# Queries turned in 32 by 32 blocks by VectorE instead of TensorE, with the order of the later batches written anew

## The chip, the cores and the metric

The kernel runs on one core of one Trainium2 chip. The metric is the device time of one execution in microseconds (us): the median of several runs, less is better. A core has five engines that each work through their own queue in order and meet only at semaphores: TensorE (PE in the profile, with its weight loads as PEld), VectorE (DVE), ScalarE (ACT), GpSimd (POOL) and SyncE (SP), which here issues nearly all DMAs.

## The reference

Two stages, all float32. First an attention through packs: 8 batches, 8 heads, 576 tokens, 64 depths, and 32 pack queries for each head.

```python
p_packed = sm_attn(p, k, v)                 # 32 packs attend to 576 tokens
out = sm_attn(q, p_packed, p_packed)        # 576 queries attend to the 32 packs
x = out.transpose(0, 2, 1, 3).reshape(B, S, H * D)
xt = x.transpose(0, 2, 1)
u = x + (xt @ U @ V).transpose(0, 2, 1)     # token mixing of rank 32
ch = np.maximum(u @ w_ch1, 0.0) @ w_ch2     # 512 -> 2048 -> 512
return u + ch
```

`sm_attn` is a softmax of `qk/8` with 1e-9 added to the sum, times the values.

## The kernel before, in words

The packs' attention over all batches comes first (the word list `opening`), mixed with the loading of weights and the first batch's products. Then batch 1 is run by a plain loop, and batches 2 to 7 by three lists of words: `prologue` once, `batch_steps` for each batch, `joint_steps` after batches 3 and 7 for the rows that four batches share. Each word names a stage and takes that stage's next piece; the program order of every engine's queue comes out of the order of these words. Nothing else orders the work: a piece whose inputs are not there holds up everything behind it on its engine.

Within a batch `batch_steps` weaves three things:

- The two large products of this batch. `H` (`half1`, lines 95 to 97) makes hidden values: six matmuls of 256 or 320 columns. `E` and `L` move them out of PSUM on ScalarE. `U` (lines 1016 to 1018) makes sums on VectorE, `C` (line 1030, ScalarE) and `D` (line 1035, VectorE) split them into a high and a low part in one of two tiles `h`, and `G` (`products`, line 1041) multiplies the parts with weights: 21 matmuls of 256 columns for a turn of four `G`. One factor of each turn, the tile `tc`, is brought from DRAM each time (`P`, line 936) into one of two rooms; the DMA waits until the turn before last has let the room go.
- The weights of the coming batch, `F0` (line 564, TensorE), `F1` and `F2` (lines 574 and 576, ScalarE and VectorE), from the tile `w1s` that `S` loads (line 556).
- The attention of the coming batch, `q..`, `s..`, `t..`, `x..`, `y..`. Its queries come in two groups of four heads (`g` is 0 or 1). For each group `load_nat` fills one tile `x`: nine tokens on a row, 64 depths each, 576 KB in one DMA (line 292). `q0`, `q1` and `q2` (`turn`, lines 303 and 306) turn them on TensorE through the identity into PSUM banks: four, four and two transposes of 128 columns. `q0a`, `q1a` and `q2a` (lines 312 and 314) copy them to the tile `xT` on ScalarE, depths on partitions. `s3` (line 323) multiplies `xT` with the packs, `s4` (line 365) turns the 32 by 32 blocks of the scores on VectorE, `s5` to `s9` are the softmax on VectorE, GpSimd and ScalarE, and `sa` (line 389) turns the result back on VectorE. There is one buffer of `xT`, which also serves `t0`, and beside the tile that a weight keeps there is one buffer of `x` for queries and for `t0` in turn.

Of the kernel before, what the change touches and what calls it, by code (L numbers as in the profile page):

```python
# [9 lines left out]
F32 = mybir.dt.float32  # L10
# [10 lines left out]
def packed_attention_mixer_kernel(  # L21
# [27 lines left out]
    nc = tc.nc  # L49
    B, H, S, D = q.shape  # L50
    NP = p.shape[2]
    R = U.shape[1]
    DM = H * D
    DF = w1.shape[1]
    P = 128
    SM = 512
    NT = 9
    I = S // NT
# [7 lines left out]
    LAST = slice(4 * I, 5 * I)  # L66
# [4 lines left out]
    U, V, w1, w2 = (a.bitcast(I32) for a in (U, V, w1, w2))  # L71
# [28 lines left out]
    pipe = ctx.enter_context(tc.tile_pool(name="pipe", bufs=1))  # L100
# [3 lines left out]
    def bank():  # L104
        return psT.tile([P, 512], F32, name="t_ps", tag="t")
# [8 lines left out]
    for z in range(2):  # L114
        a, b = (x[:, D:].rearrange("p (y z n) -> p z y n", y=2, z=2) for x in (swapped, ident))
# [15 lines left out]
    def ppT_tile():  # L131
        return pipe.tile([P, 2, P], F32, name="ppT", bufs=3)
# [4 lines left out]
    def load_ppT(b):  # L137
        ppT[b] = ppT_tile()
        nc.sync.dma_start(out=ppT[b].rearrange("p g n -> p (g n)"), in_=ppTd[b])
# [86 lines left out]
    def x_tile():  # L226
        return pipe.tile([P, 5 * 2 * P], F32, name="x", tag="x", bufs=2)
# [63 lines left out]
    def load_nat(x, src, b, g):  # L291
        nc.sync.dma_start(
            out=x.rearrange("p (h y) -> p h y", h=2),
            in_=src[b, 4 * g:4 * g + 4].rearrange("(h z) (i c) d -> (z i) h (c d)", z=2, c=NT))

    def turn(x, h, bank):

        x = x.rearrange("p (h y) -> p h y", h=2)
        t_ps = bank()
        if h < 2:  # L300
            pairs = t_ps.rearrange("p (k y a) -> p k y a", k=2, a=2)
            for j in range(4):
                nc.tensor.transpose(pairs[:, j % 2, :, j // 2], x[:, h, P * j:P * j + P], ident)  # L303
        else:
            for h in range(2):
                nc.tensor.transpose(t_ps[:64, P * h:P * h + P], x[:, h, SM:], ident)
        return t_ps
# [26 lines left out]
    def attention(b, res):  # L334

        st = {}

        def load():
            load_q(0)
            if b < 3:  # L340
                load_q(1)
            if b > 0:
                load_ppT(b)

        def load_q(g):
            st["x", g] = x_tile()[:, :2 * S]
            load_nat(st["x", g], q, b, g)

        def turn_q(g, h):
            st["t_ps", g, h] = turn(st["x", g], h, bank)  # L350
# [105 lines left out]
        def run(f, *args):  # L456
            return lambda: f(*args)

        if b != 2:
            gh = list(product(range(2), range(2)))  # L460
            return {
                "a0": [load], "a1": [run(load_q, 1)],
                **{f"q{h}": [run(turn_q, g, h) for g in range(2)] for h in range(3)},
                **{f"q{h}a": [lambda scalar, g=g, h=h: turned_q(g, h, scalar) for g in range(2)] for h in range(3)},
                "s3": [run(scores_q, g) for g in range(2)],
                "s4": [run(side, g, r) for g, r in gh],
                "s5": [run(most, g) for g in range(2)],
                "s6": [run(each, g, "m", ALU.subtract) for g in range(2)],
                "s7": [run(power, g) for g in range(2)],
                "s8": [run(total, g, k) for g in range(2) for k in range(3)],  # L470
                "s9": [run(each, g, "s", ALU.mult) for g in range(2)],
                "sa": [run(back, g) for g in range(2)],
                "t0": [room],
                "t1": [run(tokens, k) for k in (0, 2, 4)],
                "t2": [run(split_tokens, k, False) for k in (0, 2, 4)],
                "t3": [run(split_tokens, k, True) for k in (0, 2, 4)],
                "x0": [mix1], "x1": [run(split_mix1, False)], "x2": [run(split_mix1, True)],
                "y0": [run(mix2, g, hf) for hf, g in gh],
                "y1": [run(add_mix2, g, hf) for hf, g in gh],
                "y2": [run(high_mix2, g, hf) for hf, g in gh],  # L480
                "y3": [run(low_mix2, g, hf) for hf, g in gh],
                "pu": [put],
            }
# [674 lines left out]
    for word in opening.split():  # L1158
        name = word.rstrip("v") if word not in stages else word
# [7 lines left out]
        else:  # L1167
            stage()
    ahead = attention(2, res)
    ahead.pop(0)()  # L1170
    steps = ahead
    last = kept["cur"]
    now = Batch(1)
    for kt in range(NK):
# [11 lines left out]
        if kt % 4 == 2:  # L1186
            n = NPC + kt // 4 + 1
# [13 lines left out]
        c, y = divmod(kt - 1, 2)  # L1201
# [10 lines left out]
    last = now  # L1212

    prologue = (
        "a0 XG XG Hn Hn Ln En Hn En X U Ln F0n X X V C XG XMv Pn F1n XG V Sn En V Zn Hn XMv X V Hn En XMv F1n F1n Hn "
        "F2n Ln En F2n XMv Hn En Ln F2n F1n Hn En F2n Wn D En Wn U XO XO Pn XO XO Yn "
    )
    batch_steps = (
# [9 lines left out]
    )  # L1228
    joint_steps = (
# [3 lines left out]
    )  # L1233

    def each_of(f, *items):
# [4 lines left out]
    sweeps, rows = {}, {}  # L1240
# [58 lines left out]
    def run(order, without=""):  # L1299
        for word in order.split():  # L1300
            name = word if word in stages else word[:-1]
            if name[-1] == without:
                continue
            stage = next(stages[name], None)
            if stage:
                stage(*([name == word] if name in either else []))
# [40 lines left out]
```

## Time and profile before

| what | us |
|---|---|
| median of 3 runs | 778.45 (777.95 to 779.28) |
| the profiled execution | 776.24 |
| its span, first to last instruction | 774.5 |

The profile is of one execution. Its views give engine, line, operation and tiles; a busy time is the union of an engine's instructions. Matmuls overlap in the pipeline, so the time that one costs is read from the distance of starts in the timeline, not from its duration. The granted clock of TensorE was 0.997 of full speed over the span.

### The profile page before, as it was taken

Reading aid. Unit: us, or ns where it says so; the run is one execution under the profiler, and the core shown is the slowest. Engines: PE = TensorE matmul, PEld = TensorE weight load, DVE = VectorE, ACT = ScalarE, POOL = GpSimd, SP = SyncE. Lnnn points to the kernel's source line nnn. Section 1 sums busy time; section 2 is a strip of 40 time slices with the busy share of each in tenths; the row PEclk is TensorE's granted clock in tenths of the full one; section 3 lists DMA queues with packets and bytes.
Section 4 is the critical chain, followed back from the end, with each engine's and each line's share of the span. In section 5 each row is a group of like instructions: output and inputs, shape, how many; then the busy total and the mean of one; then the engine's idle time right before and its main releaser. Section 6 shows DMA issues by size and latency. Waiting matters only on the chain.

```text
span 774.5 us, 18505 instructions
## 1 busy us (share of the span) xinstructions
PE 758.3 (98%) x7280; PEld 669.7 (86%) x7280; DVE 571.4 (74%) x1209; ACT 416.4 (54%) x1034; POOL 88.3 (11%) x109
## 2 busy tenths in 40 slices
PE   8999999999999999999999999999999999999996
PEld 6666778787878899899999989998999999999996
DVE  4799799976878657856788758865886578656786
ACT  4788755553434555556554554555555555564441
POOL 1023011010101011200210002010202020200000
PEclk9999999999999999999999999999999999999998
DMA  9999985477122774566567546654656464555581
GB/s 316 346 350 297 314 213 151 124 250 255 39 82 104 244 258 107 190 206 200 164 220 224 194 143 186 195 200 152 213 146 245 149 204 146 197 176 164 164 218 61
DMA packets 105685, 151.18 MB, mean 195 GB/s; under 512 B 40448, under 2 KB 59904, under 8 KB 102016
## 3 DMA queue, kind: packets, MB, share of 16 engines
q1 hardware_dynamic: 105440, 149.75, 61.7%
q8 instruction: 57, 0.93, 0.5%
q10 hardware_dynamic: 160, 0.26, 0.1%
q14 instruction: 28, 0.23, 0.1%
HBM read 116.29 MB, written 33.69 MB: 194 GB/s over the span
## 4 chain that ended last, share of the span: by engine, by line
PE 82%; DVE 8%; ACT 4%; DMA 3%; issue 1%; POOL 0%; SPq 0%; ACTq 0%; DVEq 0%; POOLq 0%
PE o L1041 32%; PE h_ps L95 9%; PE h_ps L96 8%; PE h_ps L97 8%; PE t_ps L564 4%; PE o L95 3%; PE o L97 3%; PE o L96 3%; DVE h L1035 2%; PE o L1063 1%; PE t_ps L303 1%; DMA kx<-in_k_dram 1%; DMA bits<-in_moe_w_ch_dram 1%; PE t_ps L323 1%; ACT h L1030 1%
## 5 line engine op out<-in xcount | busy, mean ns | idle before, releaser
L1041 PE MATMUL o<-w2h,h 128*128 128x256 f32 x896 | 180.4, 281 | 0.0
L95 PE MATMUL h_ps<-ah,wth 128*128 128x256 f32 (+1 forms) x512 | 157.9, 308 | 0.4 <-ACT hj L785 0.4
L96 PE MATMUL h_ps<-al,wth 128*128 128x256 f32 (+1 forms) x512 | 150.6, 294 | 0.0
L97 PE MATMUL h_ps<-ah,wtl 128*128 128x256 f32 (+1 forms) x512 | 150.4, 294 | 0.0
L1035 DVE TENSOR_TENSOR h<-bits,h 128x896 fp32r<-128x896 f32 (+1 forms) x112 | 118.9, 1062 | 37.4 <-ACT h L1030 35.3
L1041 PEld LDWEIGHTS o<-w2h,h 128*128 128x128 f32 x896 | 146.3, 188 | 0.1
L1030 ACT CAST h<-bits 128x896 fp32r<-128x896 f32 (+1 forms) x112 | 100.4, 896 | 62.8 <-DVE bits L1018 31.5
L1041 PE MATMUL o<-w2l,h 128*128 128x256 f32 x448 | 125.3, 280 | 0.0
L95 PEld LDWEIGHTS h_ps<-ah,wth 128*128 128x128 f32 x512 | 96.3, 188 | 24.8 <-issue 10.1
L96 PEld LDWEIGHTS h_ps<-al,wth 128*128 128x128 f32 x512 | 96.4, 188 | 0.9
L97 PEld LDWEIGHTS h_ps<-ah,wtl 128*128 128x128 f32 x512 | 96.3, 188 | 0.0
L1041 PE MATMUL o<-tb,h 128*128 128x256 f32 x504 | 88.1, 281 | 0.9 <-DVE h L1035 0.9
L576 DVE TENSOR_TENSOR wtl<-t_ps,wth 128x256 fp32r<-128x256 f32 x128 | 49.4, 417 | 50.3 <-ACT wth L574 49.4
L1041 PEld LDWEIGHTS o<-w2l,h 128*128 128x128 f32 x448 | 84.2, 188 | 0.0
L1041 PEld LDWEIGHTS o<-tb,h 128*128 128x128 f32 x504 | 71.9, 189 | 2.1 <-DVE h L1035 1.7
L1006 ACT ACTIVATE bits<-h_ps 128x256 f32<-128x256 f32 x132 | 48.3, 388 | 39.4 <-PE h_ps L97 24.6
L1016 DVE TENSOR_TENSOR bits<-bits 128x256 f32<-128x256 f32 x96 | 41.4, 431 | 26.4 <-ACT bits L1006 26.3
L574 ACT CAST wth<-t_ps 128x256 fp32r<-128x256 f32 x128 | 43.3, 378 | 25.8 <-PE t_ps L564 21.1
L373 POOL TENSOR_TENSOR e<-e,m 128x576 f32<-128x576 f32 x16 | 22.7, 1418 | 286.5 <-DVE m L369 286.5
L454 POOL TENSOR_TENSOR al<-aT,ah 128x320 fp32r<-128x320 f32 (+1 forms) x32 | 32.9, 1040 | 182.8 <-ACT ah L450 154.7
L95 PE MATMUL o<-w2h,h 128*128 128x512 f32 x128 | 51.9, 406 | 0.0
L97 PE MATMUL o<-w2h,h 128*128 128x512 f32 x128 | 50.4, 394 | 0.0
(176 smaller groups left out, 1332.9 us busy)
## 6 DMA issues: line engine op xcount, KB each, us to landing
w1s<-w1D SPq DMA_DIRECT2D x24, 1024.0 KB, 6.2
tc<-tD SPq DMA_DIRECT2D x94, 256.0 KB, 3.0
bits<-in_moe_w_ch_dram SPq DMA_DIRECT2D x32, 512.0 KB, 4.6
kx<-in_k_dram SPq DMA_DIRECT2D x16, 576.0 KB, 6.4
x<-in_q_dram SPq DMA_DIRECT2D x16, 576.0 KB, 6.9
vt<-in_v_dram SPq DMA_DIRECT2D x32, 256.0 KB, 6.4
out_dram<-os SPq DMA_DIRECT2D x32, 256.0 KB, 2.8
hD<-ppall SPq DMA_DIRECT2D x30, 256.0 KB, 3.3
```

What stands on the lines that cost most here:

```text
L95: nc.tensor.matmul(ps, lhsT=lh, rhs=rh, start=start, stop=False)
L96: nc.tensor.matmul(ps, lhsT=lh, rhs=rl, start=False, stop=False)
L97: nc.tensor.matmul(ps, lhsT=ll, rhs=rh, start=False, stop=stop)
L454: nc.gpsimd.tensor_tensor(al[:, g, ns], aT[:, ns], ah[:, g, ns].bitcast(F32), op=ALU.subtract)
L564: nc.tensor.matmul(f_ps[g][xs], lhsT=ppT[b][zs, g, xs], rhs=w[zs, h // 2], start=True, stop=True)
L574: nc.scalar.copy(hi[:, g], src)
L576: nc.vector.tensor_tensor(lo[:, g], src, hi[:, g].bitcast(F32), op=ALU.subtract)
L1006: nc.scalar.activation(dst[:, 256 * (i % 2):256 * (i % 2) + 256], src, AF.Relu)
L1016: vec(l[:, 4:6], s[:, 1:3], s[:, 0:1].to_broadcast([P, 2, P]), op=ALU.add)
L1030: nc.scalar.copy(h[:, ks], src)
L1035: nc.vector.tensor_tensor(lo[:, ks], src, h[:, ks].bitcast(F32), op=ALU.subtract)
L1041: nc.tensor.matmul(ps, lhsT=a, rhs=b, start=x not in self.begun, stop=last and i == 2)
```

## The change

For batches 3 to 7 `load_blocks` replaces `load_nat`. It reads queries in pieces of one token by 32 depths (128 bytes) and lays them so that each quarter of 32 partitions holds tokens on its rows and 32 depths in its columns. A group is loaded in four steps `n`, a step in four DMAs of 256 pieces, and in the first two steps one more for the tokens that are ninth in their row: 18 DMAs a group, each of 256 pieces of 128 bytes, where one DMA of 256 pieces of 2304 bytes was before. `turn_blocks` then turns the 32 by 32 blocks on VectorE straight from `x` to `xT`: two instructions of 128 partitions by 512 elements (`qt`) and one of 64 partitions by 256 (`q9`) for each group. The transposes on TensorE, their PSUM banks and the copies on ScalarE fall away in these batches. The softmax and all products stay. Batches 0 to 2 keep the old way.

```diff
+    def load_blocks(x, b, g, n):
+        src = q[b, 4 * g:4 * g + 4].rearrange("h (f l c) (y d) -> c y l h f d", f=4, c=NT, y=2)
+        main = src[:8].rearrange("(a k r) y l h f d -> r y k a l (h f) d", a=2, k=2)
+        r, y = divmod(n, 2)
+        ps = x[32 * n:32 * n + 32]
+        for k, a in product(range(2), range(2)):
+            to = ps[:, 4 * P * k:4 * P * k + 4 * P].rearrange("(l a) (n d) -> a l n d", a=2, d=32)
+            nc.sync.dma_start(out=to[a], in_=main[r, y, k, a])
+        if r == 0:
+            rows = q[b, 4 * g:4 * g + 4].rearrange("h (f l c) (y d) -> c y l (h f) d", f=2, c=NT, y=2)
+            nc.sync.dma_start(out=ps[:, 8 * P:].rearrange("l (n d) -> l n d", d=32), in_=rows[8, y])
...
-        def load_q(g):
-            st["x", g] = x_tile()[:, :2 * S]
-            load_nat(st["x", g], q, b, g)
+        def load_q(g, n=0):
+            if b < 3:
+                x = st["x", g] = x_tile()[:, :2 * S]
+                load_nat(x, q, b, g)
+                return
+            if n == 0:
+                st["x", g] = x_tile()
+                if g == 0:
+                    load_ppT(b)
+            load_blocks(st["x", g], b, g, n)
+
+        def turn_blocks(g, last):
+            x = st["x", g]
+            if not last:
+                st["t", g] = pipe.tile([P, 4, 5 * I], F32, name="xT", bufs=1)
+                for k in range(2):
+                    nc.vector.transpose(st["t", g][:, :, P * k:P * k + P],
+                                        x[:, 4 * P * k:4 * P * k + 4 * P].rearrange("p (h n) -> p h n", h=4))
+            else:
+                nc.vector.transpose(st["t", g][:I, :, LAST], x[:I, 8 * P:].rearrange("p (h n) -> p h n", h=4))
...
-                "a0": [load], "a1": [run(load_q, 1)],
+                "a0": [load] if b < 3 else [run(load_q, 0, n) for n in range(4)],
+                "ql": [run(load_q, 1, n) for n in range(4)],
+                "qt": [run(turn_blocks, g, False) for g in range(2)], "q9": [run(turn_blocks, g, True) for g in range(2)],
...
-        "q0 H C H L G L q0a G E G E P U G N F0 N D H S H E H E F1 H F2 F1 E N F1 F2 L G F2 L C G q1 E P D H W H E F1 "
+        "H H N C N G N F0 L L D E E G U F1 F1 G N H qt H E q9 G E N H N F2 O F2 H E L P H L F1 W G F2 F1 E ql G E U C "
...
+        "G G D H S F2 Y H P E C H E L s3 L E G s4 G s4 H N P N H ql s5 E H D s6 E G L U E s7 G ql s8 G F0 s8 ql H F1 "
+        "F2 F1 G F1 F2 C W G P F1 D H L E H U L E F2 G E L U G C G F2 G s8 P qt s9 G O Plj H q9 C W D H D E s3 E A U "
```

All three lists are written anew. The first group's loads (four words `a0`) move into the end of the batch before, the second group's (four words `ql`) stand between the first group's `q9` and the second group's `qt`.

TensorE, in the batch that prepares batch 3, at the second group's queries. Before, the transposes of `q0` and `q1` stand between two products of one turn (`tb` and `tc` are weights, `h` the split values, `t_ps` the PSUM banks):

```order
L1041 MATMUL o<-w2h_120,h 128x256
L1041 MATMUL o<-tb_3389,h 128x256 x3
L303 MATMUL t_ps<-ident,x 128x128 x8
L1041 MATMUL o<-tc,h 128x256 x3
L1041 MATMUL o<-tb_3389,h 128x256 x3
```

After, TensorE meets that group only at its scores (L335 is line 323 of before, L1071 is 1041, L1093 is 1063):

```order
L97 MATMUL h_ps<-ah,wtl 128x320
L335 MATMUL t_ps<-xT,ppT 32x320
L335 MATMUL t_ps<-xT,ppT 32x256
...
L1093 MATMUL o<-ppP,aP 128x64 x16
L1071 MATMUL o<-tb_3389,h 128x256 x3
L1071 MATMUL o<-tc,h 128x256 x3
```

The eight transposes are gone from between the products, and no matmul has come in their place.

VectorE, in the same batch, at the first group. Before, sums (`bits`), the split (`h`) and the weights' low parts (`wtl`) follow each other until the scores are turned (L365):

```order
L1016 TENSOR_TENSOR bits<-bits 128x256
L1017 TENSOR_TENSOR bits<-bits 128x128
L1018 TENSOR_TENSOR bits<-bits 128x128
L1035 TENSOR_TENSOR h<-bits,h 128x896
L576 TENSOR_TENSOR wtl<-t_ps,wth 128x256 x3
L1035 TENSOR_TENSOR h<-bits,h 128x896
```

After, the queries' blocks are turned between the sums and the low parts (L1046 to L1048 are the sums, L606 is 576, L1065 is 1035):

```order
L1046 TENSOR_TENSOR bits<-bits 128x256
L1047 TENSOR_TENSOR bits<-bits 128x128
L1048 TENSOR_TENSOR bits<-bits 128x128
L372 STREAM_TRANSPOSE xT<-x 128x4x128 x2
L375 STREAM_TRANSPOSE xT<-x 64x4x64
L606 TENSOR_TENSOR wtl<-t_ps,wth 128x256 x3
L1046 TENSOR_TENSOR bits<-bits 128x256
L1047 TENSOR_TENSOR bits<-bits 128x128
L1048 TENSOR_TENSOR bits<-bits 128x128
L1065 TENSOR_TENSOR h<-bits,h 128x896
```

Three instructions have come in that write `xT`; three low parts, three sums and one split queue behind them.

SyncE, in the same batch, at the second group's loads. Before, one DMA loads the group between the stores of hidden values and the weights' stream:

```order
L963 DMA hjD_112<-aP 128x4x64
L1009 DMA hD_106<-ppall 128x512
L292 DMA x<-in_q_dram 128x2x576
L556 DMA w1s<-w1D_102 128x2048
L1009 DMA hD_106<-ppall 128x512
L936 DMA tc<-tD_139 128x512
```

After, the first step's five DMAs stand ahead of `w1s`, and thirteen more follow in one piece after two `tc` (L303 and L306 here are the DMAs of `load_blocks`; L966 is 936, L586 is 556, L1039 is 1009):

```order
L1039 DMA hD_106<-ppall 128x512
L303 DMA x<-in_q_dram 16x16x32 x4
L306 DMA x<-in_q_dram 32x8x32
L586 DMA w1s<-w1D_105 128x2048
L993 DMA hjD_112<-aP 128x4x64
L966 DMA tc<-tD_137 128x512
L966 DMA tc<-tD_138 128x512
L303 DMA x<-in_q_dram 16x16x32 x4
L306 DMA x<-in_q_dram 32x8x32
L303 DMA x<-in_q_dram 16x16x32 x8
L1039 DMA hD_106<-ppall 128x512
L966 DMA tc<-tD_139 128x512
```

Eighteen issues stand where one stood, and `w1s`, `tc` and the store `hD` queue behind them.

More of the change, by code (lines that the diff above doesn't have):

```diff
@@ L339, in load @@
             load_q(0)
-            if b < 3:
-                load_q(1)
+            load_q(1)
             if b > 0:
                 load_ppT(b)
-        def load_q(g):
-            st["x", g] = x_tile()[:, :2 * S]
-            load_nat(st["x", g], q, b, g)
+        def load_q(g, n=0):
[17 more added lines that the diff above has]
+                nc.vector.transpose(st["t", g][:I, :, LAST], x[:I, 8 * P:].rearrange("p (h n) -> p h n", h=4))
         def turn_q(g, h):
@@ L1214, in packed_attention_mixer_kernel @@
     prologue = (
-        "a0 XG XG Hn Hn Ln En Hn En X U Ln F0n X X V C XG XMv Pn F1n XG V Sn En V Zn Hn XMv X V Hn En XMv F1n F1n Hn "
-        "F2n Ln En F2n XMv Hn En Ln F2n F1n Hn En F2n Wn D En Wn U XO XO Pn XO XO Yn "
+        "a0 Hn Hn Ln F0n En XG Ln En Sn F1n U Zn Hn F1n X Hn F2n C XG En D F1n XG X En XG X V F1n V Hn V X Pn V Wn Hn "
+        "F2n Ln En XMv a0 Hn F2n Ln En F2n Hn En XMv XMv En a0 XMv U a0 Pn XO Wn XO XO XO Yn "
     )
     batch_steps = (
[9 rows of a table removed]
[9 rows of a table added]
     )
     joint_steps = (
[3 rows of a table removed]
[3 rows of a table added]
     )
```

20 rows, old and new, of tables (batch_steps, joint_steps) are left out of this document.

## The prediction

> **What bounds the kernel now.** I read the page's busy times first, then a table of stretches of 50 us, then the chain that ended last.
>
> ```profile
> PE 758.3 (98%) x7280; PEld 669.7 (86%) x7280; DVE 571.4 (74%) x1209; ACT 416.4 (54%) x1034; POOL 88.3 (11%) x109
> ...
> PE 82%; DVE 8%; ACT 4%; DMA 3%; issue 1%; POOL 0%; SPq 0%; ACTq 0%; DVEq 0%; POOLq 0%
> ```
>
> ```profile
> core 0: us, PE busy (x) PEld busy (x) DVE busy (x) ACT busy (x) POOL busy (x), PEclk, DMA share, GB/s
> 250.00:300.00 50.00, 50.00 (x441) 44.78 (x440) 32.93 (x72) 27.24 (x76) 4.19 (x3) 1.00 0.70 222
> ...
> 400.00:450.00 50.00, 49.61 (x495) 46.86 (x494) 38.53 (x88) 23.93 (x55) 4.29 (x4) 1.00 0.69 218
> ...
> 650.00:700.00 50.00, 50.00 (x456) 45.94 (x455) 32.41 (x71) 27.14 (x71) 4.30 (x4) 1.00 0.58 185
> ```
>
> A busy PE is not yet a PE at its peak, since matmuls overlap. But 82% of the chain lies on it, and where the change acts (from about 260 us on) it is idle for 0.4 us in the worst of these stretches, at the full clock (1.00). VectorE is busy 32 to 39 of 50 us there, ScalarE 24 to 27, the DMA engines 58 to 70% of the time. So what is taken out of TensorE's queue comes off the end, as long as nothing else arrives later than now.
>
> **What the change removes.** The transposes after 240 us are those of batches 3 to 7:
>
> ```profile
> L303 PE MATMUL t_ps<-ident,x x80: 271/272/273, 262.1 to 629.9; 128*128 128x128 f32 x80
> ```
>
> Their duration of 272 ns is not their price. That is read from the starts in TensorE's timeline (start, duration):
>
> ```profile
> 272.21 0.60 PE L303 MATMUL t_ps<-ident,x 128*128 128x128 f32 x4
> 272.57 0.36 PE L95 MATMUL h_ps<-ah,wth 128*128 128x256 f32 x1
> 272.77 0.28 PE L96 MATMUL h_ps<-al,wth 128*128 128x256 f32 x1
> 272.89 0.28 PE L97 MATMUL h_ps<-ah,wtl 128*128 128x256 f32 x1
> ...
> 275.86 0.38 PE L306 MATMUL t_ps<-ident,x 128*64 128x128 f32 x2
> 275.99 0.36 PE L1041 MATMUL o<-w2h,h 128*128 128x256 f32 x1
> 276.20 0.28 PE L1041 MATMUL o<-w2l,h 128*128 128x256 f32 x1
> ```
>
> ```profile
> 289.81 1.03 PE L303 MATMUL t_ps<-ident,x 128*128 128x128 f32 x8
> 290.60 0.48 PE L1041 MATMUL o<-tc,h 128*128 128x256 f32 x2
> ```
>
> Four transposes hold the queue from 272.21 to 272.57, 0.36 us. The matmul behind them then takes 0.20 until the next starts, where an undisturbed one takes 0.12 (272.77 to 272.89): going from float32 to the split kind costs 0.08 more. So a group of four costs 0.44. Two of L306 cost 0.13 and 0.09 (275.99 to 276.20 less 0.12), 0.22. Eight in one piece cost 0.79, and 0.08 behind them, 0.87. A batch has two fours, one eight and two pairs: 2 x 0.44 + 0.87 + 2 x 0.22 = 2.19 us. Five batches (80 transposes of the first kind, 16 in each) make 10.95, say 11.0 us. Of the matmuls that stay, none is added, and the other places where float32 and split products meet keep their number.
>
> The Trainium skill, page "TensorE: Matmul & The Clock Gate", section "Back-to-back issue gap", gives about 81 ns for a sustained weight load and matmul of 128 columns; by that the hundred would be worth 8.1 us. The rows give 90 ns in a group and the 0.08 behind it, and I go by the rows.
>
> The copies on ScalarE go too, and the queries stop using PSUM banks:
>
> ```profile
> L312 ACT COPY xT<-t_ps 128x512 f32<-128x512 f32 x30 | 17.2, 592 | 15.3 <-PE t_ps L303 15.0
> L314 ACT COPY xT<-t_ps 64x256 f32<-64x256 f32 x16 | 5.8, 365 | 3.0 <-PE t_ps L306 2.9
> ```
>
> Four of 592 ns and two of 365 are 3.1 us of ScalarE in a batch. It is half idle; I count nothing for this.
>
> **What it adds on VectorE.** For each group two turns of 128 x 512 and one of 64 x 256. The nearest rows:
>
> ```profile
> L389 DVE STREAM_TRANSPOSE aT<-e 128x576 f32<-128x576 f32 x16 | 12.3, 771 | 7.6 <-POOL e L373 7.5
> ...
> L365 DVE STREAM_TRANSPOSE e<-t_ps 128x256 f32<-128x256 f32 x16 | 6.5, 406 | 0.0
> ```
>
> L389 also goes from SBUF to SBUF: 512/576 of 771 is 0.69 us; two of L365 would be 0.81, the upper end. The small one lies between 256/576 of 771, 0.34, and 0.41. I take 0.69 and 0.36: 1.7 us a group, 3.5 a batch, 17 in all (20 by the upper ends). In 50 us that is about 2.2 more, and 38.5 becomes 40.7: VectorE doesn't become the bound by its sum. It also has gaps that such a piece fits into:
>
> ```profile
> 266.25 0.43 DVE L1016 TENSOR_TENSOR bits<-bits 128x256 f32<-128x256 f32 x1 [2.33 <-ACT bits L1006]
> ...
> 278.44 0.85 DVE L365 STREAM_TRANSPOSE e<-t_ps 128x320 f32<-128x320 f32 x2 [2.79 <-PE t_ps L323]
> ```
>
> I cost it at nothing. The cover is these gaps; if it is gone, up to 1.7 us a group lands on TensorE (first rival). The change also adds a wait there: the turn waits for the last DMA of its group, and the low parts L576, the sums L1016 and the split L1035 queue behind it. TensorE waits for the split (`G`) and the low parts (`H`).
>
> **What it adds on SyncE and the DMA engines.** Eighteen issues a group for one:
>
> ```profile
> L950 SPq DMA_DIRECT2D ppP<-ppD x24: 303/430/1157, 260.2 to 685.7; - x24
> DMA to landing us min/median/max: 1.8/2.2/5.6
> ```
>
> ```profile
> L292 SPq DMA_DIRECT2D x<-in_q_dram x10: 469/539/2548, 251.3 to 620.8; - x10
> DMA to landing us min/median/max: 5.7/6.0/7.7
> ```
>
> L950, 32 KB in pieces of 256 bytes, is nearest: 0.43 us an issue, so 7.7 a group and 15.5 a batch, less 1.1 for the two of L292. SyncE mostly waits. One row alone:
>
> ```profile
> SPq L936 <- PE o L1041: 143.4, 58, 7.1
> ```
>
> So there is time for the issues; only their place matters. The packs' load `ppT` goes out with the group's first step, one issue as before. Behind the 13 in one piece (13 x 0.43 = 5.6 us) stand `hD` and `tc`; `w1s` stands behind five (2.2 us). What the pieces cost on the DMA engines:
>
> ```profile
> DMA packets 105685, 151.18 MB, mean 195 GB/s; under 512 B 40448, under 2 KB 59904, under 8 KB 102016
> ...
> q1 hardware_dynamic: 105440, 149.75, 61.7%
> ...
> hjD<-aP SPq DMA_DIRECT2D x24, 128.0 KB, 3.3
> ...
> tD<-ta SPq DMA_DIRECT2D x7, 256.0 KB, 2.8
> ```
>
> 10 groups of 18 x 256 are 46,080 packets of 128 bytes in place of 2,560. An average packet takes 61.7% of 774.5 x 16 us over 105,440: 73 ns. That is the upper end, 46,080 x 73 / 16 = 210 us an engine over five batches. The lower end is no cost, as the bytes are the same. `hjD` (512 pieces of 256 bytes) lands 0.5 us after `tD` (128 of 2 KB) would, and 24 more pieces an engine in 0.5 us are 21 ns each: 60 us an engine over some 400 us, 0.15 on a share of 0.6. I take that value; it is of the same kind. The engines don't fill.
>
> **The order made anew.** All else that moves keeps its count. Its cost is unknown from both sides. Today's order leaves TensorE some waits that a better one could save, and a worse one adds to:
>
> ```profile
> PEld o L1041 <- DVE h L1035: 3.8, 10, 0.7
> ```
>
> I take zero, with 2 us either way.
>
> **Sum.** The profiled execution took 776.24 (span 774.5, 1.7 around it). Less 11.0 it is 765.2. The median of the runs stands 2.2 above the profiled one, so the forecast is 778.45 - 11.0 = 767.4. About 0.2%, 1.6 us, is what a measurement of this kernel can tell from no change.
>
> **The rivals.**
>
> *VectorE is late in part.* The splits come just in time already; the chain around 300 us:
>
> ```profile
> 299.44 0.95 ACT h L1030
> 300.39 0.02 issue
> 300.42 1.78 DVE h L1035
> 302.19 0.04 issue
> 302.24 0.86 PE o L1041 x5
> ```
>
> Here TensorE waits for VectorE. A turn of 1.7 us ahead of a split with no gap moves it onto TensorE. If a fifth to a half of the ten groups' 17 us does, 3.5 to 8.7 us of the gain go: 771 to 776. For it: `h` has two tiles, so a split cannot run far ahead. Against: gaps of over 2 us, and a ScalarE that is relieved. Chance 0.15.
>
> *The pieces come late: slower.* The place is the second group's `qt`. Between the last `ql` and it the list has six `G` and three `H`, some 31 and 18 matmuls of about 0.12, roughly 6 us. Four issues (1.7) and a landing of 2.2 make 3.9, in time by 2. If the landing is as the old loads', 6.0 to 7.7 us, or worse, VectorE stands 1.7 to 3.4 us in each of five batches. Just-in-time `h` hands this to TensorE. The gain is 2.2 us a batch, so it decides from a landing of 6.6 us. With the `tc` behind 13 issues late by another 2 us, a batch loses 4 to 5: 778.45 - 11 + 20 to 25, 787 to 792; barely past the point, 780. For it: L950's longest landing, 5.6. Against: its median. Chance 0.13.
>
> *Small pieces are slow by rule.* At the upper end, 73 ns a packet, the DMA engines would need 0.6 x 400 + 210 = 450 us in 400: DMA-bound, some 40 us slower, 807. The Trainium skill, page "DMA: Bandwidth & Descriptors", section "Specifications", asks for at least 512 bytes for line rate and has smaller writes read, changed and written back, which speaks against this change. By `hjD` such pieces are cheap here, though no run shows 128 bytes. Chance 0.03.
>
> *Nothing gained.* The freed time only makes TensorE wait at the next just-in-time split: 778. Against it stands a TensorE without idle time. Chance 0.05.
>
> **The numbers.** The forecast has 0.64, with its own range from 765 to 770 (2 us of order either way). With the late VectorE nearly all on the faster side, faster has 0.78, same 0.06 (nothing gained, and an edge of its neighbours), slower 0.16. For 8 in 10 the range takes in the forecast and VectorE late: 764 to 777.
>
> **What would show it.** Right: 7,180 matmuls on PE, no L303 on `x` after 240 us, PE busy about 747, VectorE up by 17 us, ScalarE down by about 15, about 149,000 packets, PE still idle for no more than 0.5 us in 50. A turn of 512 elements near 0.69 us. Wrong: PE waiting for `h` L1065 far above 3.8 us; VectorE waiting for the DMA of `x` ahead of its turns; `tc` or `w1s` named as what TensorE waits for; a DMA share near 1.

## The result and the profile after

| kernel | median us (lowest to highest) | ratio to before, 95% interval |
|---|---|---|
| before | 777.83 (777.14 to 779.28, 15 runs) | |
| changed | 781.8 (779.18 to 786.5, 15 runs) | 1.0055 [1.0041, 1.0069] |

The changed kernel is about 4 us slower, 14.4 above the forecast. Its profiled execution took 779.18 (span 777.3), the lowest of its fifteen, so its rows show too little of the loss, not too much.

The page's busy times, the chain by engine, the packets and the main DMA queue:

```profile
PE 751.1 (97%) x7180; PEld 660.4 (85%) x7180; DVE 590.7 (76%) x1235; ACT 401.9 (52%) x1008; POOL 95.3 (12%) x109
...
DMA packets 151928, 151.21 MB, mean 195 GB/s; under 512 B 89248, under 2 KB 108704, under 8 KB 148256
...
q1 hardware_dynamic: 151680, 149.76, 64.7%
...
PE 74%; DVE 9%; DMA 8%; ACT 4%; issue 2%; SPq 1%; POOL 1%; ACTq 0%; POOLq 0%; DVEq 0%
```

The hundred transposes are gone (7,180 matmuls), VectorE has 19 us more and ScalarE 14.5 less, as announced. But TensorE's share of the chain fell from 82 to 74%, and DMA rose from 3 to 8%. The stretches of 50 us say where:

```profile
250.00:300.00 50.00, 45.48 (x349) 40.21 (x348) 32.74 (x71) 23.47 (x69) 3.10 (x2) 0.97 0.69 193
400.00:450.00 50.00, 48.08 (x480) 45.24 (x465) 40.43 (x89) 24.71 (x58) 4.95 (x4) 1.00 0.72 210
650.00:700.00 50.00, 50.00 (x449) 46.87 (x448) 36.55 (x80) 26.04 (x67) 4.88 (x4) 1.00 0.59 183
```

From 250 to 300 us TensorE gets through 349 matmuls where before it got through 441. The later stretches are nearly whole. The first residual sums of batch 2 and of batch 4 (o<-ppP,aP, first and last start) mark the same sums in every kernel, before in the first fence, after in the second:

```profile
L1063 PE MATMUL o<-ppP,aP x32: 270/270/318, 293.8 to 294.7; 32*128 32x64 f32 x32
...
L1063 PE MATMUL o<-ppP,aP x32: 270/270/318, 474.6 to 475.5; 32*128 32x64 f32 x32
```

```profile
L1093 PE MATMUL o<-ppP,aP x32: 270/270/318, 300.8 to 301.7; 32*128 32x64 f32 x32
...
L1093 PE MATMUL o<-ppP,aP x32: 270/270/318, 480.7 to 481.5; 32*128 32x64 f32 x32
```

At batch 2's residual the changed kernel is already 7.0 us late. (Its order has some other work ahead of these sums; the same order with relieved loads, below, reaches them at 293.8 too.) Two batches and the joint rows further on, it has gained 0.9 back (180.8 us before, 179.9 after), where 4.4 was to be had.

The chain in that window, in order of time (start, duration, what; "issue" is time with no visible wait):

```profile
264.97 0.59 SPq L303
265.56 0.04 issue
265.61 0.65 SPq L303
...
267.61 0.60 SPq L306
268.20 0.04 issue
268.25 1.65 SPq L303
...
273.86 0.61 SPq L303
274.47 0.04 issue
274.51 2.83 DMA tc<-tD
277.34 0.04 issue
277.38 3.54 PE o L1071 x18
280.93 0.21 PE h_ps L95
281.14 0.21 PE h_ps L96
```

This chain runs through the queue of SyncE. Thirteen loads of query blocks go out one after the other, 0.61 us each, from 264.97 to 274.47; behind them stands the DMA of `tc`, and TensorE waits for it. VectorE and TensorE in the same window (in brackets the idle time before and what ended it):

```profile
274.90 0.71 DVE L372 STREAM_TRANSPOSE xT<-x 128x512 f32<-128x512 f32 x1 [7.00 <-DMA x<-in_q_dram]
```

```profile
277.38 0.62 PE L1071 MATMUL o<-tc,h 128*128 128x256 f32 x3 [3.76 <-DMA tc<-tD]
```

VectorE stands 7.0 us at the first turn, because the loads that it needs are still being issued; TensorE stands 3.8 us for a `tc` that couldn't be issued. Once issued, that `tc` took 2.83 us, no more than the median of all `tc` (3.1): it went out late, it did not travel slowly. The stand also cost more than its length, since the granted clock (the last figure but two) was low behind it:

```profile
274.00:278.00 4.00, 0.62 (x5) 0.62 (x6) 2.42 (x6) 0.45 (x2) 0.00 (x0) 1.00 0.68 199
278.00:282.00 4.00, 4.00 (x24) 4.00 (x23) 2.82 (x6) 1.75 (x4) 0.00 (x0) 0.57 0.99 307
```

At 0.57 of full speed 4 us hold the work of 2.3, so some 1.7 us come on top of the 3.8: together 5.5 of the 7.0 that the kernel is late at batch 2's residual. The instructions themselves, over the whole run (minimum, median, maximum in ns):

```profile
L303 SPq DMA_DIRECT2D x<-in_q_dram x160: 577/607/1646, 255.1 to 629.0; - x160
```

```profile
L372 DVE STREAM_TRANSPOSE xT<-x x20: 654/670/714, 274.9 to 633.0; 128x512 f32<-128x512 f32 x20
```

```profile
L375 DVE STREAM_TRANSPOSE xT<-x x10: 394/395/398, 276.8 to 633.6; 64x256 f32<-64x256 f32 x10
```

The turns took about what was said (0.67 and 0.40 us, 0.69 and 0.36 said). An issue took 0.61, not 0.43.

### The profile page after: what moved, and what is told of

Its sections match the earlier page's. It is cut to its first block, busy times and chain, and to the rows that moved or that the text cites. A ratio compares the mean times of both kernels' runs of the same rounds, so it can differ in the third digit from the quotient of the medians.

```text
span 777.3 us, 18562 instructions
## 1 busy us (share of the span) xinstructions
PE 751.1 (97%) x7180; PEld 660.4 (85%) x7180; DVE 590.7 (76%) x1235; ACT 401.9 (52%) x1008; POOL 95.3 (12%) x109
## 3 DMA queue, kind: packets, MB, share of 16 engines
q1 hardware_dynamic: 151680, 149.76, 64.7%
## 4 chain that ended last, share of the span: by engine, by line
PE 74%; DVE 9%; DMA 8%; ACT 4%; issue 2%; SPq 1%; POOL 1%; ACTq 0%; POOLq 0%; DVEq 0%
PE o L1071 29%; PE h_ps L95 8%; PE h_ps L96 7%; PE h_ps L97 7%; PE t_ps L594 3%; PE o L95 3%; PE o L97 3%; PE o L96 3%; DVE h L1065 2%; DMA bits<-in_moe_w_ch_dram 2%; ACT h L1060 2%; DMA kx<-in_k_dram 2%; PE o L1093 1%; POOL e L401 1%; DMA aP<-aD 1%
## 5 line engine op out<-in xcount | busy, mean ns | idle before, releaser
L1071 PE MATMUL o<-w2h,h 128*128 128x256 f32 x896 | 181.4, 282 | 0.0
L95 PE MATMUL h_ps<-ah,wth 128*128 128x256 f32 (+1 forms) x512 | 154.6, 302 | 0.2 <-ACT hj L815 0.2
L1065 DVE TENSOR_TENSOR h<-bits,h 128x896 fp32r<-128x896 f32 (+1 forms) x112 | 114.8, 1029 | 46.2 <-ACT h L1060 45.9
L1071 PEld LDWEIGHTS o<-w2h,h 128*128 128x128 f32 x896 | 147.3, 189 | 0.0
L1071 PE MATMUL o<-w2l,h 128*128 128x256 f32 x448 | 126.0, 281 | 0.0
L1071 PE MATMUL o<-tb,h 128*128 128x256 f32 x504 | 90.9, 287 | 1.9 <-DVE h L1065 1.1
L1071 PEld LDWEIGHTS o<-w2l,h 128*128 128x128 f32 x448 | 84.7, 189 | 0.0
L1071 PEld LDWEIGHTS o<-tb,h 128*128 128x128 f32 x504 | 71.9, 189 | 14.6 <-issue 5.9
L606 DVE TENSOR_TENSOR wtl<-t_ps,wth 128x256 fp32r<-128x256 f32 x128 | 49.9, 417 | 37.3 <-ACT wth L604 36.3
L482 POOL TENSOR_TENSOR al<-aT,ah 128x320 fp32r<-128x320 f32 (+1 forms) x32 | 35.8, 1131 | 176.3 <-ACT ah L478 148.2
L1071 PE MATMUL o<-tc,h 128*128 128x256 f32 x282 | 50.0, 286 | 5.3 <-DMA tc<-tD 5.3
```

Source lines behind the costliest of these rows:

```text
L95: nc.tensor.matmul(ps, lhsT=lh, rhs=rh, start=start, stop=False)
L482: nc.gpsimd.tensor_tensor(al[:, g, ns], aT[:, ns], ah[:, g, ns].bitcast(F32), op=ALU.subtract)
L606: nc.vector.tensor_tensor(lo[:, g], src, hi[:, g].bitcast(F32), op=ALU.subtract)
L1065: nc.vector.tensor_tensor(lo[:, ks], src, h[:, ks].bitcast(F32), op=ALU.subtract)
L1071: nc.tensor.matmul(ps, lhsT=a, rhs=b, start=x not in self.begun, stop=last and i == 2)
```

## The experiments

The theory after the result: SyncE issues in program order, each block load holds it 0.6 us, and 36 a batch in place of two delay the queries and the `tc` behind them. The first rival: the 128-byte pieces load the DMA engines or land late. The second: VectorE's turns, or the order written anew, hold up just-in-time splits. Unless said otherwise each kernel is the changed one with one edit; "before" is the kernel before on the same chip, with medians of 777.47 to 778.17.

### Plain loads, for all batches and for batch 3 alone

```diff
-        for k, a in product(range(2), range(2)):
-            to = ps[:, 4 * P * k:4 * P * k + 4 * P].rearrange("(l a) (n d) -> a l n d", a=2, d=32)
-            nc.sync.dma_start(out=to[a], in_=main[r, y, k, a])
+        flat = q[b, 4 * g:4 * g + 4].rearrange("h s d -> (h s d)")
+        if n == 0:
+            nc.sync.dma_start(out=x[:, :8 * P], in_=flat[:8 * P * P].rearrange("(p y) -> p y", p=P))
+        elif n == 1:
+            nc.sync.dma_start(out=x[:64, 8 * P:], in_=flat[8 * P * P:].rearrange("(p y) -> p y", p=64))
```

> Each group's queries come by two DMAs of long rows (128 rows of 4096 bytes at the first of the four steps, 64 rows of 1024 at the second) in place of 18 of 128-byte pieces; the bytes, the turns on VectorE and the new order stay. What the blocks then hold is not the queries' layout, so the output is not the reference's. SyncE theory (the issues of the pieces, 0.6 us each, hold up the weights tc and the queries themselves): the loss goes, 765 to 770 us, no wait of VectorE for x. VectorE theory (the turns and the new order make splits late): stays at 778 or above. Pieces theory (128-byte packets slow the DMA engines): 765 to 770 as well.

Measured: 773.59 (771.78 to 774.08), ratio 0.9942 [0.9928, 0.9957]. Of VectorE's 7.8 us of waiting for `x` 0.2 is left. The loss is gone, but the time stays 3.6 us above the range that was expected; the runs with copies and with the old order, further down, take that up. The same in batch 3 alone:

> The same two long DMAs a group, for batch 3 alone; batches 4 to 7 keep their pieces (batch 3's output is then not the reference's). SyncE theory: up to the first residual some 9 us are lost in the changed kernel, because there the list puts 18 issues into the short prologue; most of it returns, 772 to 775 us. Pieces theory: a fifth of the packets goes, so a fifth of the loss, 778 to 780. VectorE theory: no change, 780 to 783.

Measured: 775.0 (773.47 to 778.54), ratio 0.9967 [0.9952, 0.9983]. So the block loads cost 8.2 us, and batch 3 alone accounts for 6.8 of them. This takes away issues, pieces and part of the wait at once; the next runs part these.

### The same pieces, issued by GpSimd

```diff
-            nc.sync.dma_start(out=to[a], in_=main[r, y, k, a])
+            nc.gpsimd.dma_start(out=to[a], in_=main[r, y, k, a])
```

(and the same for the small one.)

> The changed kernel with the 36 block loads of a batch issued by GpSimd instead of SyncE; same packets, same order of words. SyncE theory: SyncE is free again and tc comes in time; if GpSimd, busy 12% so far, issues them at 1 us or less each, 766 to 772 us. Pieces theory and VectorE theory: no change, 780 to 783. If GpSimd needs much over 1 us for an issue, its softmax steps get late and all theories give a slower kernel.

Measured: 772.77 (772.22 to 773.41), ratio 0.9936 [0.9921, 0.9951]: 9.0 us better than the changed kernel, with the same loads at the same places of the list. It beats both kernels. The issues on GpSimd and the stretch from 250 to 300 us:

```profile
L303 POOL DMA_DIRECT2D x<-in_q_dram x160: 562/562/719, 244.5 to 620.7; - x160
```

```profile
250.00:300.00 50.00, 49.69 (x434) 44.10 (x433) 37.30 (x79) 25.69 (x74) 19.51 (x32) 1.00 0.77 220
```

An issue is no cheaper there (0.56 us). But GpSimd had little to do, and nobody's `tc` stands behind it. TensorE gets through 434 matmuls again.

One thing besides the issuer changed. The profile books these loads on a queue of their own, as 5,760 packets of 1 KB on average, where the changed kernel's main queue had 48,960 packets more than here:

```profile
q1 hardware_dynamic: 102720, 143.85, 60.6%
q0 software_dynamic: 5760, 5.91, 4.3%
```

So the count of packets can't be compared between the two. Their time can: 64.9% of 771.3 us on both queues is 501 us an engine, against 503 in the changed kernel (64.7% of 777.3). Nor do the loads land sooner. First the changed kernel, then this one:

```profile
DMA to landing us min/median/max: 2.1/2.9/8.4
DMA to landing us min/median/max: 1.9/3.7/9.3
```

The DMA engines worked as long as before, they were busier in this stretch (0.77 against 0.69), the loads took longer to land, and yet the loss is gone. So neither the load on the engines nor a slow landing is its cause.

### Half of the issues on GpSimd

```diff
-            nc.sync.dma_start(out=to[a], in_=main[r, y, k, a])
+            (nc.sync if r == 0 else nc.gpsimd).dma_start(out=to[a], in_=main[r, y, k, a])
```

> The changed kernel, but the DMAs of each group's third and fourth step (eight of eighteen) are issued by GpSimd; ten a group stay on SyncE. Pieces, places in the list and results are those of the changed kernel. If SyncE's issues cost the time, and cost it in proportion, the time lies between none on SyncE (772.8) and all eighteen (781.8): about 777.5; if it is the longest run of issues in one piece ahead of a tc that decides (13 become 5 on SyncE), nearly all comes back: 772.5 to 775. If it is the pieces on the DMA engines, nothing changes: 780 to 783.

Measured: 776.36 (774.68 to 779.08), ratio 0.9984 [0.9971, 0.9997]. With none, ten and eighteen issues a group on SyncE the time is 772.8, 776.4 and 781.8. The interval, 775.6 to 777.6, lies just below strict proportion (777.8) and above what was expected if only the longest run of issues in one piece counted (772.5 to 775). So the number of issues counts, not that run alone.

### Twice as many issues for the same pieces

```diff
-            nc.sync.dma_start(out=to[a], in_=main[r, y, k, a])
+            for z in range(2):
+                ns = slice(8 * z, 8 * z + 8)
+                nc.sync.dma_start(out=to[a][:, ns], in_=main[r, y, k, a][:, ns])
```

> Each of the 16 main DMAs of a group is cut in two of 128 pieces: the same packets and bytes, 34 issues a group in place of 18. SyncE theory: 34 issues of about 0.43 us are 14.6 us a group where 18 of 0.61 are 11.0; 3 to 4 us more in the prologue and some in each batch, 786 to 800 us. Pieces theory and VectorE theory: no change, 780 to 783.

Measured: 874.77 (870.88 to 879.47), ratio 1.125 [1.1206, 1.1294]. Direction as the theory has it, size far beyond: I had taken half as many pieces to be issued faster. They are not:

```profile
L305 SPq DMA_DIRECT2D x<-in_q_dram x320: 577/598/1732, 255.4 to 718.8; - x160
```

```profile
DVE xT L374 <- DMA x<-in_q_dram: 52.8, 12, 15.8
```

0.598 us with 128 pieces, 0.607 with 256: between these two the price is per DMA. The 34 issues of a group are 20 us of SyncE, and VectorE's waits for `x` reach 15.8 us. The 160 DMAs that came in are 160 x 0.598 = 96 us more of SyncE, and the kernel got 93 slower: with the queue full, about as much as it grew by reached the end.

### Plain loads at a late place

The two plain loads at the third and fourth step instead of the first and second:

```diff
-        if n == 0:
+        if n == 2:
...
-        elif n == 1:
+        elif n == 3:
```

> As the plain loads (two DMAs of long rows a group), but issued at the third and fourth of the four steps, so that the queries are asked for as late as in the changed kernel while SyncE has two issues in place of 18. SyncE theory: the issues ahead of the queries, not their place in the list, made them late: within 1 us of the plain loads, 773 to 775. Rival (the list asks for them too late whatever they cost): VectorE waits for x, 777 or more.

Measured: 772.67 (771.0 to 773.38), ratio 0.9927 [0.9906, 0.9949]. Even as the last to go out the loads are in time: no wait of VectorE for `x` shows. The first residual sums of batch 2, in the changed order, now start 7.0 us earlier:

```profile
L1088 PE MATMUL o<-ppP,aP x32: 270/270/318, 293.8 to 294.7; 32*128 32x64 f32 x32
```

So it isn't where the list puts the loads, but how long the queue takes to get through them.

### The second tc earlier

In the prologue the second `Pn` moves right behind the first. Before, thirteen block loads stood between the two.

```diff
-        ... X Pn V Wn Hn F2n Ln En XMv a0 ... XMv U a0 Pn XO Wn ...
+        ... X Pn Pn V Wn Hn F2n Ln En XMv a0 ... XMv U a0 XO Wn ...
```

> The changed kernel, loads on SyncE, with one word moved in the prologue: the load of the second tc stands right behind the first, ahead of the three loads of queries that it followed. If tc behind the 13 issues is what costs in the prologue, TensorE's wait of 3.8 us and the half clock behind it go: 776 to 778.5. If the queries themselves come too late (VectorE stood 7 us for x and the splits behind it), little is won: 779.5 to 782.

Measured: 782.27 (778.58 to 784.83), ratio 1.0047 [1.0024, 1.007]: no gain. TensorE's waits after 240 us (the profiled execution is the slowest of eight, 784.83):

```profile
PE h_ps L95 <- ACT bits L1036: 3.2, 1, 3.2
PE o L1071 <- DVE h L1065: 2.5, 5, 0.6
PE o L1071 <- DMA tc<-tD: 2.3, 1, 2.3
```

`tc` was only what ended last. With it early, VectorE still stands 8.1 us for `x`, ScalarE stands 5.1 for VectorE's low parts behind the turn, and TensorE waits 3.2 for a bank that ScalarE has yet to clear. To shorten one wait in an ordered queue did nothing while the queue itself was full.

### The transposes put back

With the loads on GpSimd, the 100 transposes of `x` are issued on TensorE again, at `qt` and `q9`, into a bank that nobody reads.

```diff
+            for h in range(2, 3) if last else range(2):
+                t_ps = bank_k()
+                for j in range(2 if last else 4):
+                    src = x[:, 64 * j:64 * j + 64] if last else x[:, SM * h + P * j:SM * h + P * j + P]
+                    nc.tensor.transpose(t_ps[:src.shape[1], P * j:P * j + P], src, ident)
```

> The GpSimd variant with the ten transposes a group put back on TensorE beside VectorE's turns, into a PSUM bank that nobody reads: no copy, no use, a hundred in all. The step of the forecast that priced them at 0.44 for four and 0.22 for two, 11.0 us in all, expects 772.8 + 11 = 782 to 785, a little more where TensorE now meets the queries' landing. Rival (TensorE has hidden room in the new order, so that their removal was worth much less): under 779.

Measured: 787.87 (786.62 to 789.79), ratio 1.0128 [1.0104, 1.0152]: 15.1 us above the same kernel without them, and 2.9 above the range. Their removal isn't hollow. Why it is 15 and not 11 is open: of three groups of eight two held the queue for 0.79 us, as in the prediction's rows, and one for 1.05, and TensorE's waits grew by less than 1 us.

### Copies on ScalarE in place of the turns

The relieved kernels stand at 772.7, some 5.8 above 777.9 - 11.0 = 766.9. Is it VectorE's turns, or the new order? In the kernel with the late plain loads:

```diff
-                    nc.vector.transpose(st["t", g][:, :, P * k:P * k + P],
+                    nc.scalar.copy(st["t", g][:, :, P * k:P * k + P],
...
-                nc.vector.transpose(st["t", g][:I, :, LAST],
+                nc.scalar.copy(st["t", g][:I, :, LAST],
```

> The kernel with plain loads late in the list (two long-row DMAs a group, at steps 3 and 4), and the turns of qt and q9 are now copies of the same size on ScalarE instead of block turns on VectorE, at the same places of the list. The queries are not turned, so the attention's numbers are not the reference's; instructions of all other kinds keep their number. The plain late loads gave 772.7, some 5 above the forecast. If VectorE's turns keep it from the forecast (17 us of VectorE in front of just-in-time splits), the time falls to 767 to 770. If the list's new order does, it stays at 771.5 to 774 with VectorE's busy time down by 17 us.

Measured: 772.75 (771.67 to 773.72), ratio 0.9936 [0.9916, 0.9956], with VectorE relieved as meant:

```profile
PE 748.8 (97%) x7180; PEld 658.7 (86%) x7180; DVE 575.6 (75%) x1205; ACT 414.7 (54%) x1038; POOL 98.0 (13%) x109
```

14.3 us less VectorE than with the turns (589.9), and no change in time. In the new order the turns cost no more than these copies.

### The old order without transposes

The kernel before, its one load a group and its list, but from batch 3 on `turn_q` does nothing, and `turned_q` takes `x` itself, once by ScalarE and once by VectorE:

```diff
+            ps, xs = (P, slice(P * h, P * h + P)) if h < 2 else (I, LAST)
+            src = st["x", g][:ps, 4 * P * h:4 * P * h + 4 * P] if h < 2 else st["x", g][:ps, 14 * I:]
+            nc.scalar.copy(st["t", g][:ps, :, xs], src.rearrange("p (h n) -> p h n", h=4))
```

> The kernel before, with its own order and its one plain load a group, but for batches 3 to 7 the transposes of the queries on TensorE are left out, and ScalarE's copies at q0a, q1a and q2a take the untransposed queries from the tile x. The queries are not turned, so the attention's numbers are not the reference's; the count of matmuls is that of the changed kernel. With relieved SyncE the changed kernel stands at 772.7, 5 above the forecast. If the list written anew costs those 5 us, the old list without transposes comes out at 766 to 769. If the hundred transposes are worth no more than 5 where they stood, since the next just-in-time wait takes the rest, it is 771.5 to 774.

Measured: 769.16 (768.86 to 770.65), ratio 0.9885 [0.9868, 0.9903]. The old order gets 8.8 us out of the same removal (7.5 to 10.3 by the interval), the new one 5.2. TensorE's waits after 240 us are short:

```profile
PE t_ps L323 <- ACT xT L361: 1.5, 4, 0.4
PE o L1047 <- DVE h L1041: 0.8, 3, 0.4
```

The second kernel has `nc.vector.transpose` in place of `nc.scalar.copy`:

> As the old order with copies on ScalarE, but VectorE turns the 32 by 32 blocks of x into xT at the places q0a, q1a and q2a, in pieces of 128 x 512 twice and 64 x 256 once a group, as in the changed kernel. The blocks come from plain rows, so the numbers are not the reference's. If VectorE's turns cost nothing beside this order, the time is that of the copies on ScalarE within 1 us (766 to 769). If they hold up the splits, it is 1.7 us or more a batch above them, up to 8 us (over 770).

Measured: 777.34 (774.77 to 783.97), ratio 1.0006 [0.9982, 1.003]. The profiled execution, its fastest (774.77), has one wait of TensorE that stands out:

```profile
PE t_ps L323 <- DVE xT L361: 7.8, 5, 1.8
```

In the old order the scores follow straight on the turn, and TensorE waits for VectorE 1.6 us a batch: 6.3 more than for ScalarE's copy, of the 5.9 between the two profiled executions. The rest up to 8.2 between the medians shows in no profile here.

### Where the new order loses 3.6 us

Four more runs on the kernel with loads on GpSimd looked for the place. First, TensorE waits for the aligned sums `aT` (L417) 3.5 us, 0.7 a batch. One `G` was moved ahead of `t1`:

```diff
-        ... U t1 M t1 t2 G C G t3 ...
+        ... U G t1 M t1 t2 C G t3 ...
```

> The GpSimd variant with one word moved in each batch: the product G that stands behind the first two t1 now stands ahead of the first. Order theory (of the 6 us that the GpSimd variant is short of the sum, TensorE's wait of 0.7 us in each of five batches for the attention's last turn on VectorE, L417, is 3.5): that wait goes and the median falls by 2 to 3.5 us against the GpSimd variant, to 769 to 771. Rival (the splits of VectorE are the limit anyway, the wait only moves): within 0.7 us of the GpSimd variant, 772 to 773.5.

Measured: 773.3 (771.4 to 774.8), ratio 0.9942 [0.9923, 0.9961]: that wait halved (1.7), and from batch 2's residual to batch 3's it still took 78.0 us. Then lists of the kernel before were put back where no query stands in them: `joint_steps`, the batch steps for the last batch alone, and both lists for the last batch.

```diff
-        "ZJ Hn N G Ln C G Hn PJ D RJ G U G G U C G G D PJ G RJ N RJ F0n C G D G G PJ U G RJ G U C G G D PJ G U G C G "
+        "ZJ F0n C N Hn D G G U G PJ U G RJ RJ G C G G D PJ G Hn RJ C G G D G PJ U G U G C G G D PJ G RJ N Sn G C U G "
...
```

> The changed kernel with its loads issued by GpSimd, and of the three lists the last one, joint_steps, is put back to that of the kernel before; it holds no queries in either form, and takes the same number of every other piece. Prologue and batch steps are the changed ones. If the list written anew costs about 3 us and most of that lies after batch 7, where TensorE waits for the split h four times between 720 and 726 us, the time falls by 1.5 to 3 from 772.8: 769.8 to 771.3, and the time from the last batch's second residual to the end shrinks by about 2. If the waits there only move on to the next turn, it stays at 772 to 773.5.

Measured: 774.8 (773.0 to 776.93), ratio 0.9965 [0.9953, 0.9977]: 2 us slower than without this edit, above both ranges. The waits for the split that were meant to go stayed: I had misplaced them, they stand in the batch steps.

```diff
-        run(batch_steps, "n" if joint_next else "j")
+        steps = batch_steps if b < B - 1 else " ".join(w for w in last_steps.split() if w[0] not in "qa")
+        run(steps, "n" if joint_next else "j")
```

> The changed kernel with its loads issued by GpSimd (772.8), and for the last batch alone the batch steps of the kernel before in place of the new ones. That batch prepares no coming batch, so it holds no queries and no turns in either order, and takes the same number of every other piece. Putting the joint list back gained nothing, since TensorE's four waits for the split h at 720 to 726 us stand between the last batch's two residuals, in the batch steps. If those waits are what the new order costs there, they go, and the time falls by 1.5 to 2.5: 770.3 to 771.3. If they only move on, it stays at 772 to 773.5.

Measured: 773.09 (772.02 to 774.58), ratio 0.994 [0.9925, 0.9955]. TensorE's waits between 662 and 757 us:

```profile
PE o L1071 <- DMA tc<-tD: 1.6, 1, 1.6
PE o L1071 <- DVE h L1065: 0.2, 1, 0.2
```

All but 0.2 us of the waits for the split went (1.2 before), and one for `tc` took their place. With the last batch's joint list put back as well:

```diff
-            run(joint_steps, "" if b < B - 1 else "n")
+            run(joint_steps if b < B - 1 else last_joint, "" if b < B - 1 else "n")
```

> The changed kernel with its loads issued by GpSimd (772.8), and for the last batch both lists, batch steps and joint steps, are those of the kernel before. Putting back the batch steps alone took the waits for the split h away and brought one wait of 1.6 us for tc. From the last batch's first residual to its last, the old order without transposes takes 93.9 us where the new order takes 95.2. If the last batch of the new lists costs that by itself, 1 to 2 us come back: 770.5 to 771.8. If its cost depends on what the batches ahead leave behind (where the DMAs of tc and the splits stand when it begins), it stays at 772 to 773.5.

Measured: 773.78 (770.42 to 774.76), ratio 0.9944 [0.9927, 0.9962]; again a wait for `tc`, 1.3 us. The tail of the old order doesn't pay behind the new batches. That the new order, with its two plain loads a group, costs 3.6 us against the old one is measured. In the profiled executions TensorE's waits after 240 us add up to 6.8 in the kernel with loads on GpSimd and to 2.3 in the old order without transposes, so idle time of TensorE goes along with the loss. Which words of the list make it stays open: the largest wait, 3.5 for `aT`, could be halved without gain.

## Why the prediction was wrong, point by point

The medians add up, each kernel against its neighbour:

| step | us | change |
|---|---|---|
| before | 777.9 | |
| no transposes, old order (copies on ScalarE) | 769.2 | -8.8 |
| the same in the new order, plain loads | 772.75 | +3.6 |
| turns on VectorE instead of copies | 772.67 | -0.1 |
| 18 block loads a group, issued by GpSimd | 772.77 | +0.1 |
| the same loads issued by SyncE: the change | 781.8 | +9.0 |

- **Transposes, 11.0.** Measured 8.8 in their old places, and 1.5 more went into the new wait for the copies: the price was about right there. Put back at other places they cost 15.1, so a price read at one place is not yet that of another. The estimate by the Trainium skill's page "TensorE: Matmul & The Clock Gate", section "Back-to-back issue gap", was 8.1; the interval, 7.5 to 10.3, holds that and not 11.0, as long as the new wait counts against the gain.
- **VectorE at nothing.** Right in the new order, by the run with copies. It isn't right by itself: at the old places the turns cost 8.2, of which 6.3 show as TensorE waiting at the scores right behind them. "The cover is these gaps" hid that the order made the cover, and that it has a price.
- **SyncE at nothing: the step that failed.** "SyncE mostly waits", "there is time for the issues; only their place matters". The row behind it, 143.4 us of waiting, is a sum over the whole run, and waiting behind the place of the new issues is no room for them. SyncE in the kernel before, at the end of the prologue:

```profile
265.25 1.18 SPq L1009 DMA_DIRECT2D hD<-ppall  x2
...
272.46 0.44 SPq L1009 DMA_DIRECT2D hD<-ppall  x1
280.01 0.32 SPq L936 DMA_DIRECT2D tc<-tD  x1
```

Twelve DMAs went out from 265.25 to 272.90 with no more than half a microsecond between two rows of that stretch; the pause of 7.1 us comes after them. In the changed kernel thirteen loads stand in just this stretch (264.97 to 274.47), and SyncE issues them without a pause while VectorE and TensorE wait. And 0.43 us an issue came from a simpler DMA: 36 issues of 0.61 are 22 us a batch, not 15.5. The cost, 9.0 us, was larger than what the removal won.
- **Pieces on the DMA engines.** Said: 21 ns a piece, 60 us an engine, no stall. The queue's share went from 61.7% of 774.5 us to 64.7% of 777.3, 25 us an engine more, so less; 12 ns a packet by the estimate at the end. That the engines don't fill was right: issued by GpSimd, these loads cost 0.1 us against plain rows. The Trainium skill's page "DMA: Bandwidth & Descriptors", section "Specifications", asks for at least 512 bytes a transfer for full rate; whatever rate the pieces of 128 bytes had, it cost this kernel no time.
- **Order at 0 with 2 us either way.** 3.6, outside its bound. With SyncE relieved of the loads the kernel still stood 5.4 above the forecast: 3.6 of it lies here and 2.2 in the transposes, less 0.5 since the kernel before now stood at 777.9 and not at 778.45.
- **The rivals.** "The pieces come late" named the right victims, the turn and the `tc` behind 13 issues, and by its sign it happened. Its place was the second group's `qt` in each of five batches and its measure a landing of 6.6 us. What happened was the first group's turn, once, at the end of the prologue, whose last 13 issues also stand in one piece ahead of a `tc`; and it came from the time to issue. I had counted the last four issues ahead of a turn, not all 13. "VectorE late in part" did not happen: TensorE's weight loads waited 4.6 us for `h`, 3.8 before. Nor did "nothing gained": the old order without transposes is 8.8 faster.

The Trainium skill's page "Perfetto Trace Analysis", section "DMA Optimizations", says that it may help to balance DMAs over the engines that can issue them where an issuing engine is solid with them. These runs agree: 9.0 us. Its section "What 'DMA-bound' means" asks for larger descriptors in that case. No run here tried larger ones in the same number of DMAs; half as many in a DMA left the issue at 0.6 us. What helped were fewer DMAs, or another issuer.

## What to carry to other kernels

Count the DMAs that a change adds, not only their bytes: each held its issuing engine for some 0.6 us here, with 128 pieces as with 256, and everything that stood behind it in that queue waited as well. Whether the issuer has time is read in the very stretch where the new issues stand, from its own rows there; a total of waiting over the run doesn't say where the waiting lies. And where an order is written anew beside a change, measure the order alone and the change alone, since each can hide the price of the other.

## What the runs showed of the hardware

- An issue's time did not depend on the number of pieces: 0.598 us for 128 and 0.607 for 256 on SyncE, 0.562 for 256 on GpSimd, each a pattern of three dimensions; rows of a simpler pattern (the prediction's L950) took 0.43. That the pattern makes this difference is not shown.
- 128-byte pieces were cheap on the DMA engines. With the loads on GpSimd, 48,960 packets left the main queue, 46,080 of them such pieces, and 35.5 us an engine with them (64.7% of 777.3 less 60.6% of 771.3): 16 x 35.5 / 48,960 = 12 ns each, an estimate from these shares.
- The same loads issued by GpSimd were booked as 5,760 packets, with 33 us an engine (4.3% of 771.3). A count of packets is no measure of the pieces there.
- After TensorE had stood for 3.76 us, its matmuls started 0.21 us apart (280.93, 281.14) where 0.12 is usual, and the granted clock was 0.57 over the next 4 us (278 to 282). With `tc` early it stood for 3.2 us, and the clock was 0.52 from 282 to 285. A stand of this length cost nearly half as much again.
- The changed kernel's fifteen runs spread over 7.3 us, the fifteen of the kernel before over 2.1. The old order with turns on VectorE, with no block loads at all, spread over 9.2 in ten runs. Why is open.
